# Attention ahead of a balanced mixture of experts: the order of tiles, q and loads, and where x waits

## The chip, the cores and the metric

The kernel runs on one core of one Trainium2 chip. The metric is the time of one execution on the device in microseconds (us), the median of several runs. Engines are named as in the profile: PE is TensorE (PEld its weight loads), ACT is ScalarE, DVE is VectorE, POOL is GpSimd, SP issues most of the DMAs.

## The reference

```
q, k, v: (8 batches, 8 heads, 576, 64) f32;  g_norm: (64,)
kv  = sum over s of k[s, d] v[s, e]              # per batch and head, 64 x 64
o   = q kv
x   = o / sqrt(mean(o*o over the head's 64) + 1e-6) * g_norm
x   -> (4608 tokens, 512): a token is (batch, s), its row the 8 heads side by side

logits = x w_gate                                # 8 experts
go through all (token, expert) pairs by falling logit; a token goes to the first
expert that still has room, each expert takes 4608 / 8 = 576 tokens
out[token] = relu(x[token] w1[e]) w2[e]          # w1: 512 x 1024, w2: 1024 x 512 per expert
```

## The kernel before

The work has three stages: the attention (to about 125 us), a search for the first expert's tokens (to about 160 us), and the eight experts, one after the other, with the search for the next ones beside them. The diff touches the first stage alone.

**Loads.** `load(name, b, h)` fetches one of k, v, q for batch `b` and half `h` of its heads, 576 KB (589,824 bytes), on SP's queue. Each name and half has two buffers, so a load for batch `b + 2` waits until PE has read the one of batch `b`. `paced` adds a dependence: a load or a write of x is not issued before the third one ahead of it has landed. SP issues in the order of the program. The first two batches are loaded at the start in the order k v q, k v q; later ones come from `again(names, h)` inside `prepare`.

**prepare(b)** is a generator that makes batch `b` ready in steps, which the tiles of batch `b - 1` are put between:

- `sum_kv(r)`: 18 products of 64 x 64 per pair of heads, into one PSUM tile `kv_ps`; ACT copies one half out (`odd`), DVE adds (`kv`), POOL copies it to both halves of `kvx`;
- `turn_q(n)`, n = 0 to 4: four blocks of q (two for n = 4) are transposed by PE into a PSUM tile `qt_ps`; DVE copies n = 1 and 2 to `qt`, ACT the others;
- `t_ps`: kv transposed by PE, copied by ACT to `kvt`; `w_ps`: kv times g_norm and w_gate, copied by DVE into the last columns of `kvx`, so that one product gives the attention's output and its share of the logits.

`qt_ps`, `t_ps` and `w_ps` share two PSUM buffers (tag `tr`). `qt` and `kvx` have three buffers each in SBUF.

**ones(n)** issues n products of a bf16 tile of ones, 512 columns, into a PSUM tile that is written over afterwards; they compute nothing that is used. There are 18 at the start, 5 in the preparation of batch 0, two ahead of each later `sum_kv`, and in every batch one ahead of tile 0 and two ahead of tile 3.

**tiles.** Batch `b` has four tiles of 128 tokens, and the odd batches a fifth one, made of the last 64 tokens' blocks of both batches of the pair (its products write 64 partitions each, hence `o_ps` x32 in the profile, where other tiles show x16). `one(t, ...)` computes a tile: products of `qt` and `kvx` into `o_ps` (two PSUM buffers), ACT's square `sq` and copy `o_sb`, and DVE's sum `ms`. After a batch's tiles, `scale()` gives `inv`, and `logits()` the logits `lg` of its tokens. x itself (`xo` = `o_sb` times `inv`) is made by POOL, one operation per tile, if the tile is `own`, else by ACT in eight operations per tile, which the list `late` puts behind the whole attention. `last_own = GC - (R + 1) // 2` makes the last batch's five tiles the late ones. The writes of `xo` to `x_dram` are held in `writes` and issued when eight or more are waiting; `xo` has five buffers.

**chores** are pieces of DVE work for the search (its constants, then for each quarter of the tokens `mx`, `pick`, `code_mx`, `best` and the comparison `over_c`), put in one by one after some tiles and at the end of a batch.

The order on PE, DVE, ACT and SP in this stage is that of the program (`manual_schedule`). The search that follows is a serial chain of DVE comparisons and PE counts (`given_ps`). At its end come the list of the first expert's tokens (`rel_s`, `ids`) and POOL's gather `xg` of their rows from `x_dram`. POOL's order is written out too: a small gather `rows_first` stands ahead of it, which waits for the last write of x.

Of the kernel before, what the change touches and what calls it, by code (L numbers as in the profile page):

```python
# [7 lines left out]
FT = mybir.dt.float32  # L8
# [7 lines left out]
P = 128  # L16
# [10 lines left out]
def kernel(  # L27
# [14 lines left out]
    B, H, S, D = q.shape  # L42
# [4 lines left out]
    HP = P // 2  # L47
    R = S // HP
# [39 lines left out]
            loaded[name, b, h].rearrange("p r j d -> p r (j d)"),  # L88
            src[b].rearrange("h s d -> (h s) d").rearrange("(r p j) d -> p r (j d)", r=NP, j=R)[:, rs]))

    for b in range(2):
        for h in range(2):
            for name in "kvq":
                load(name, b, h)

    ones_b = asg.tile([P, P], BF, name="ones_b")
    nc.vector.memset(ones_b, 1.0)
# [254 lines left out]
    def chore(times=1):  # L352

        for _ in range(times):
            if chores:
                chores.pop(0)()
# [12 lines left out]
    def prepare(b):  # L369

        k_sb, v_sb, q_sb = ([loaded.pop((name, b, h)) for h in range(2)] for name in "kvq")
        q_sb = [x.rearrange("p r j d -> p (r j d)") for x in q_sb]
        NT = NP * R // 2
        qt = att.tile([P, 2, NT, HP], FT, name="qt", tag="qt", bufs=3)
        turned_q[b] = qt

        def turn_q(n):
            m = min(4, NT - 4 * n)
            t_ps = psa.tile([P, 4, P], FT, name="qt_ps", tag="tr", bufs=2)
            for x in range(m):  # L380
                h, at = divmod(4 * n + x, NT // 2)
                nc.tensor.transpose(t_ps[:, x, :], q_sb[h][:, at * P:(at + 1) * P], ident)  # L382

            to, got = qt[:, :, 4 * n:4 * n + m], t_ps[:, 0:m].rearrange("p x (l c) -> p l x c", l=2)
            if n in (1, 2):
                nc.vector.tensor_copy(to, got)
            else:
                nc.scalar.copy(to, got)


        kv_ps = psa.tile([P, 2, 512], FT, name="kv_ps", tag="kv")

        def sum_kv(r):
            for j in range(R):
                for l in range(2):
                    ls, cs = slice(l * D, (l + 1) * D), slice(j % 2 * D, (j % 2 + 1) * D)
                    nc.tensor.matmul(kv_ps[cs, l, r * D:(r + 1) * D], lhsT=k_sb[r // 2][ls, r % 2, j, :], rhs=v_sb[r // 2][ls, r % 2, j, :],  # L397
                                     start=(j < 2), stop=(j >= R - 2))

        def again(names, h):  # L400
            if b + 2 < B:
                for name in names:
                    load(name, b + 2, h)

        if b > 0:
            ones(2, kv_ps[:, 0, :])
        for r in range(2):
            sum_kv(r)
            if r:
                again("kv", 0)  # L410
            turn_q(r)
            yield
        sum_kv(2)
        sum_kv(3)
        again("kv", 1)
        odd = att.tile([D, 2, NP * D], FT, name="odd", tag="odd")
        nc.scalar.copy(odd, kv_ps[D:P, :, 0:NP * D])
        kv = att.tile([D, NP, 2, D], FT, name="kv", tag="kv")
        nc.vector.tensor_tensor(kv.rearrange("p r l d -> p l r d"),  # L419
                                kv_ps[0:D, :, 0:NP * D].rearrange("p l (r d) -> p l r d", d=D),  # L420
                                odd.rearrange("p l (r d) -> p l r d", d=D), op=AL.add)

        kvx = att.tile([P, H, W], FT, name="kvx", tag="kvx", bufs=3)
        for n in range(2):
            nc.gpsimd.tensor_copy(kvx[n * D:(n + 1) * D, :, 0:D], kv.rearrange("p r l d -> p (r l) d"))  # L425
        if b == 0:
            ones(5)
        yield
        turn_q(2)
        again("q", 0)  # L430
        t_ps = psa.tile([P, NP, D], FT, name="t_ps", tag="tr", bufs=2)
        for r in range(NP):
            nc.tensor.transpose(t_ps[:, r, :], kv[:, r].rearrange("p l d -> p (l d)"), ident[0:D, 0:D])
        kvt = att.tile([P, NP, D], FT, name="kvt", tag="kvt")
        nc.scalar.copy(kvt, t_ps)
        yield
        turn_q(3)
        if b == 0:
            nc.vector.tensor_scalar(gw.rearrange("p r l e -> p (r l e)"), in0=gw.rearrange("p r l e -> p (r l e)"),
                                    scalar1=g_col, scalar2=None, op0=AL.mult)  # L440
        w_ps = psa.tile([P, NP, 2 * E], FT, name="w_ps", tag="tr", bufs=2)
        for r in range(NP):
            for n in range(2):
                nc.tensor.matmul(w_ps[n * D:(n + 1) * D, r], lhsT=kvt[:, r, :],
                                 rhs=gw[:, r].rearrange("p l e -> p (l e)"), start=True, stop=True)
        nc.vector.tensor_copy(kvx[:, :, D:W], w_ps.rearrange("p r (l e) -> p (r l) e", l=2))
        kv_of[b] = kvx
        turn_q(4)
        again("q", 1)

    LAG = 4
    writes, late = [], []
    last_own = GC - (R + 1) // 2

    def tiles(c0, rows):


        T = len(rows)
        o_sb = att.tile([P, T, H, W], FT, name="o_sb", tag="o_sb", bufs=2)
        xo = att.tile([P, T, H, D], FT, name="xo", tag="xo", bufs=LAG + 1)  # L460
        ms = att.tile([P, T * H], FT, name="ms", tag="ms")
        rt = att.tile([P, T * H], FT, name="rt", tag="rt")
        inv = att.tile([P, T * H], FT, name="inv", tag="inv")
        own = c0 + T <= last_own

        def one(t, copies, fill):

            o_ps = psa.tile([P, 2, 512], FT, name="o_ps", tag="o", bufs=2)
            ones(fill, o_ps[:, 0, :])
# [16 lines left out]
            sq = att.tile([P, H, D], FT, name="sq", tag="sq")  # L486
            nc.scalar.activation(sq.rearrange("p (b h) d -> p b h d", b=2), o4[:, :, :, 0:D], ACT.Square, scale=D ** -0.5)  # L487
            copies.append(lambda: nc.scalar.copy(o_sb[:, t].rearrange("p (b h) w -> p b (h w)", b=2), o_ps[:, :, 0:NP * W]))  # L488
            if own or t != T - 2:
                while copies:  # L490
                    copies.pop(0)()
            nc.vector.reduce_sum(out=ms[:, t * H:(t + 1) * H], in_=sq, axis=AXX)  # L492
# [38 lines left out]
    with tc.manual_schedule(engines={PE, DVE, ACTE, SPE}):  # L531
        ones(18)
        for _ in prepare(0):
            pass
        for b in range(B):
            parts = prepare(b + 1) if b + 1 < B else iter(())
            rows = [((b, j), (b, j + 2)) for j in (0, 1, 4, 5)]
            if b % 2:
                rows.append(((b - 1, R - 1), (b, R - 1)))
            one, scale, logits = tiles(b // 2 * R + b % 2 * (R // 2), rows)  # L540
            copies = []
            if b in choose_at:
                early(*choose_at[b])
            for t in range(len(rows)):
                one(t, copies, {0: 1, 3: 2}.get(t, 0))
                next(parts, None)
                if b < 2 or t == 3 or b == 6 and t == 2:
                    chore()
            for _ in parts:
                pass  # L550
            if b + 1 == B:
                while chores:
                    chore()
            scale()
            logits()
            if b < B - 1:
                chore(2 if b == 6 else 1)

            while len(writes) >= 2 * LAG:
                writes.pop(0)()  # L560
        early(27, GC)
        while chores:
            chore()
        for do in late:
            do()
        while writes:
            writes.pop(0)()
# [765 lines left out]
```

## Time and profile before

| | |
|---|---|
| median of 3 runs | 655.35 us (655.14 to 655.75) |
| the profiled execution | 656.87 us, its span 655.1 us |
| mean granted clock of PE | 0.964 |
| PE busy | 607.8 us, 93% of the span |
| DVE, POOL, ACT busy | 59%, 60%, 30% |
| moved by DMA | 91.02 MB, 139 GB/s over the span |
| last o_ps of the attention | 122.51 us |
| first gather of x (xg) | 155.30 us |

The profile is of one execution, by the hardware profiler. Its page gives the busy share of each engine in 40 slices of the span (a digit is tenths), the clock that PE was granted, the DMA engines' share, and the chain of work that ended last. The trace behind it gives timelines: start and length in us, the operation, and in brackets how long the engine had been idle before it and what ended that. A line with xN stands for N instructions; an f32 product of the program shows as two of them.

### The profile page before, as it was taken

How to read it: one execution, taken by the hardware profiler on the slowest of the kernel's cores; microseconds unless marked ns; L12 is line 12 of the kernel's file. 1: busy time of each engine (PE TensorE's matmuls, PEld its weight loads, DVE VectorE, ACT ScalarE, POOL GpSimd, SP SyncE). 2: the span in 40 equal slices, each digit the busy share in tenths (PEclk: the TensorE clock that was granted, in tenths of full speed). 3: DMA queues.
4: the chain of work that ended last, by engine and by line, in shares of the span. 5: the costliest groups of instructions: out<-in, count | busy, mean ns of one | idle time of the engine just before them, and what ended most of it. 6: DMA issues, size and time to landing. Idle time of an engine off the chain costs nothing.

```text
span 655.1 us, 12759 instructions
## 1 busy us (share of the span) xinstructions
PE 607.8 (93%) x4922; PEld 467.4 (71%) x4939; DVE 385.8 (59%) x1242; ACT 195.0 (30%) x397; POOL 391.1 (60%) x407
## 2 busy tenths in 40 slices
PE   7889999346999999999999999999999999999994
PEld 4767777343778678867877786778678867877873
DVE  4456767877788678578747955975771153123101
ACT  1545556631331223123212322221223123222310
POOL 1134544204586488659747973887388579848822
PEclk9979999756999999999999999999999999999998
DMA  8998988324506403620631082109104520820001
GB/s 271 315 313 293 309 300 320 126 83 144 185 2 232 137 34 109 220 74 1 213 125 66 2 291 70 42 5 325 41 33 128 203 72 1 292 77 34 0 10 64
DMA packets 49884, 91.02 MB, mean 139 GB/s; under 512 B 3744, under 2 KB 20128, under 8 KB 49824
## 3 DMA queue, kind: packets, MB, share of 16 engines
q1 hardware_dynamic: 43200, 71.31, 31.8%
q0 software_dynamic: 5920, 18.88, 8.4%
q8 instruction: 39, 0.64, 0.4%
q14 instruction: 21, 0.17, 0.1%
q10 hardware_dynamic: 704, 0.02, 0.1%
HBM read 71.32 MB, written 18.87 MB: 138 GB/s over the span
## 4 chain that ended last, share of the span: by engine, by line
PE 77%; DVE 8%; DMA 6%; issue 4%; ACT 2%; POOL 1%; POOLq 0%; SPq 0%; DVEq 0%; ACTq 0%
PE x_ps L1149 13%; PE x_ps L1109 12%; PE z_ps L1149 9%; PE y_ps L1149 9%; PE y_ps L1109 8%; PE z_ps L1109 7%; DMA v_sb<-in_v_dram 4%; PE o_ps L481 4%; PE y_ps L1211 4%; PE t_ps L1051 3%; PE kv_ps L397 3%; PE qt_ps L382 2%; PE given_ps L658 1%; PE given_ps L653 1%; DMA q_sb<-in_q_dram 1%
## 5 line engine op out<-in xcount | busy, mean ns | idle before, releaser
L1154 ACT COPY h<-x_ps 128x288 f32<-128x288 f32 x93 | 37.2, 400 | 166.1 <-PE x_ps L1149 159.7
L1149 PE MATMUL x_ps<-xs,sw 128*128 128x288 f32 x248 | 71.4, 409 | 0.4 <-DVE xs L1064 0.4
L1076 POOL DMA_INDIRECT out_dram<-y_sb,outs x32 | 31.5, 983 | 56.6 <-DVE y_sb L1247 41.1
L1109 PE MATMUL x_ps<-tw,sh 128*128 128x256 f32 x256 | 61.5, 384 | 0.0
L1149 PEld LDWEIGHTS x_ps<-xs,sw 128*128 128x128 f32 x248 | 46.1, 190 | 13.4 <-issue 1.0
L1056 ACT ACTIVATE xt<-t_ps,g_col 128x512 f32<-128x512 f32 (+3 forms) x41 | 25.8, 635 | 91.1 <-PE t_ps L1051 90.9
L1101 POOL TENSOR_TENSOR sh<-hid 128x512 f32<-128x512 f32 x32 | 40.7, 1273 | 19.9 <-ACT hid L1124 19.9
L1109 PEld LDWEIGHTS x_ps<-tw,sh 128*128 128x128 f32 x256 | 47.0, 190 | 7.0 <-issue 0.8
L1037 POOL TENSOR_TENSOR sw<-w_sb 128x256 f32<-128x256 f32 x64 | 46.8, 731 | 7.9 <-PE z_ps L1149 7.5
L513 POOL TENSOR_TENSOR xo<-o_sb,inv 128x512 f32<-128x512 f32 x31 | 32.9, 1091 | 30.7 <-DVE inv L500 17.5
L1124 ACT ACTIVATE hid<-hid 128x576 f32<-128x576 f32 x64 | 43.8, 686 | 22.6 <-DVE hid L1163 12.6
L959 POOL DMA_INDIRECT xg<-x_dram,ids x40 | 37.9, 947 | 15.5 <-issue 9.8
L481 PE MATMUL o_ps<-kvx,qt 64*128 64x72 f32 (+1 forms) x640 | 39.7, 273 | 5.3 <-ACT o_sb L488 3.4
L1187 POOL TENSOR_TENSOR tw<-w_sb 128x512 f32<-128x512 f32 x32 | 40.1, 1277 | 6.5 <-DMA w_sb<-in_moe_w_dram 6.5
L481 PEld LDWEIGHTS o_ps<-kvx,qt 64*128 64x128 f32 (+1 forms) x640 | 34.4, 180 | 12.9 <-issue 8.1
L1149 PE MATMUL z_ps<-xt,sw 128*128 128x288 f32 x128 | 38.0, 414 | 0.0
L1149 PE MATMUL x_ps<-xt,w_sb 128*128 128x288 f32 x124 | 37.3, 415 | 0.5 <-ACT xt L1056 0.5
L1149 PE MATMUL y_ps<-xt,w_sb 128*128 128x288 f32 x128 | 36.8, 408 | 0.0
L1149 PE MATMUL z_ps<-xs,sw 128*128 128x288 f32 x128 | 36.8, 409 | 0.0
L1149 PE MATMUL y_ps<-xs,w_sb 128*128 128x288 f32 x128 | 36.5, 407 | 0.0
L492 DVE TENSOR_REDUCE ms<-sq 128x8 f32<-128x512 f32 x36 | 24.3, 682 | 20.4 <-ACT sq L487 20.1
L425 POOL COPY kvx<-kv 64x512 f32<-64x512 f32 x16 | 9.7, 608 | 44.2 <-DVE kv L419 24.7
(307 smaller groups left out, 1336.1 us busy)
## 6 DMA issues: line engine op xcount, KB each, us to landing
w_sb<-in_moe_w_dram SPq DMA_DIRECT2D x32, 512.0 KB, 5.5
w_sb<-in_moe_w_dram SPq DMA_DIRECT2D x8, 2048.0 KB, 12.6
k_sb<-in_k_dram SPq DMA_DIRECT2D x16, 576.0 KB, 5.5
v_sb<-in_v_dram SPq DMA_DIRECT2D x16, 576.0 KB, 5.9
q_sb<-in_q_dram SPq DMA_DIRECT2D x16, 576.0 KB, 5.6
x_dram<-xo SPq DMA_DIRECT2D x16, 512.0 KB, 4.3
x_dram<-xo SPq DMA_DIRECT2D x4, 256.0 KB, 3.7
xg<-x_dram,ids POOLq DMA_INDIRECT x40, 5.0
```

Source lines behind the costliest of these rows:

```text
L481: nc.tensor.matmul(o_ps[rows_at, rp, (2 * r2 + l) * W:(2 * r2 + l + 1) * W], lhsT=turned_q[bn][ks, l, block // 2:block // 2 + m].rearrange ...
L513: nc.gpsimd.tensor_tensor(xo[:, t], o_sb[:, t, :, 0:D], inv[:, t * H:(t + 1) * H].rearrange("p (h o) -> p h o", o=1).to_broadcast([P, H, D ...
L959: tokens = nc.gpsimd.indirect_dma_start(out=xg[0:nr], out_offset=None, in_=x_dram, in_offset=bass.IndirectOffsetOnAxis(ap=ids[0:nr, n:n + ...
L1037: in_order(nc.gpsimd.tensor_tensor(o, x, y, op=op))
L1076: put = nc.gpsimd.indirect_dma_start(out=out, out_offset=bass.IndirectOffsetOnAxis(ap=ids_of[t][0:nr, n:n + 1], axis=0), in_=y_sb[0:nr, :] ...
L1101: in_order(nc.gpsimd.tensor_tensor(o[:, ms], x[:, ms], y[:, ms], op=op))
L1109: nc.tensor.matmul(p_ps[:, n], lhsT=left[:, f, n * P:(n + 1) * P], rhs=right[:, f], start=first, stop=(f == FH - 1), skip_group_check=True)
L1124: nc.scalar.activation(both, both, ACT.Relu)
L1149: nc.tensor.matmul(p_ps, lhsT=lhs[:, r], rhs=rhs[:, r], start=(m in (1, 2, 4, 5) and r == 0), stop=(r == 1), skip_group_check=(m in (6, 7, ...
L1154: nc.scalar.copy(u, p_ps)
L1187: in_order(nc.gpsimd.tensor_tensor(o, x, y, op=AL.subtract))
L1211: nc.tensor.matmul(y_ps[l * nr:(l + 1) * nr], lhsT=hid[:, l * FH + f, a:a + nr], rhs=w2[:, l * FH + f, :], start=(f == 0), stop=(f == FH - 1))
```

## The change

- The second batch's loads come in the order k v k v q q. In `prepare`, q is turned one step later than before (for b > 0): the sums of two pairs of heads fill the first step, group 0 of q comes in the second, groups 1 and 2 right behind `t_ps` in the third, 3 and 4 around `w_ps`. As before, the loads of q are asked for after groups 2 and 4.
- In odd batches the short tile, which also reads the batch before, goes first. `qt` and `kvx` get two buffers instead of three.
- Ones: in tiles only one each ahead of the first and the fourth tile of batches 0 to 2. In the preparation of batch 0 there are 8 more, in that of the last batch 3.
- x: `xo` has six buffers instead of five. The writes of batches 0 to 4 are issued together at the end of batch 4, behind all loads, those of batch 5 at its end, the rest after the attention. `last_own` makes batch 6 late too, so ACT makes nine tiles of x instead of five, POOL 27 instead of 31.
- The chores are put elsewhere: in batch 6 one after every tile, so that none is left for batch 7; in batches 2 to 5 after the second and fourth tile, and at the end of a batch only up to batch 3.

```diff
--- before.py
+++ after.py
@@ -88,10 +88,9 @@
             loaded[name, b, h].rearrange("p r j d -> p r (j d)"),
             src[b].rearrange("h s d -> (h s) d").rearrange("(r p j) d -> p r (j d)", r=NP, j=R)[:, rs]))
 
-    for b in range(2):
-        for h in range(2):
-            for name in "kvq":
-                load(name, b, h)
+    for b, order in enumerate(("kvqkvq", "kvkvqq")):
+        for n, name in enumerate(order):
+            load(name, b, int(name in order[:n]))
 
     ones_b = asg.tile([P, P], BF, name="ones_b")
     nc.vector.memset(ones_b, 1.0)
@@ -371,7 +370,7 @@
         k_sb, v_sb, q_sb = ([loaded.pop((name, b, h)) for h in range(2)] for name in "kvq")
         q_sb = [x.rearrange("p r j d -> p (r j d)") for x in q_sb]
         NT = NP * R // 2
-        qt = att.tile([P, 2, NT, HP], FT, name="qt", tag="qt", bufs=3)
+        qt = att.tile([P, 2, NT, HP], FT, name="qt", tag="qt", bufs=2)
         turned_q[b] = qt
 
         def turn_q(n):
@@ -402,14 +401,25 @@
                 for name in names:
                     load(name, b + 2, h)
 
+        turns = [[0], [1], [2], [3], [4]] if b == 0 else [[], [0], [1, 2], [3], [4]]
+
+        def turn_some():
+            for n in turns.pop(0):
+                turn_q(n)
+                if n in (2, 4):
+                    again("q", n // 2 - 1)
+
         if b > 0:
             ones(2, kv_ps[:, 0, :])
-        for r in range(2):
-            sum_kv(r)
-            if r:
-                again("kv", 0)
-            turn_q(r)
-            yield
+        sum_kv(0)
+        sum_kv(1)
+        again("kv", 0)
+        if b == 0:
+            ones(2)
+        turn_some()
+        yield
+        if b == 0:
+            ones(6)
         sum_kv(2)
         sum_kv(3)
         again("kv", 1)
@@ -420,21 +430,23 @@
                                 kv_ps[0:D, :, 0:NP * D].rearrange("p l (r d) -> p l r d", d=D),
                                 odd.rearrange("p l (r d) -> p l r d", d=D), op=AL.add)
 
-        kvx = att.tile([P, H, W], FT, name="kvx", tag="kvx", bufs=3)
+        kvx = att.tile([P, H, W], FT, name="kvx", tag="kvx", bufs=2)
         for n in range(2):
             nc.gpsimd.tensor_copy(kvx[n * D:(n + 1) * D, :, 0:D], kv.rearrange("p r l d -> p (r l) d"))
+        turn_some()
         if b == 0:
             ones(5)
         yield
-        turn_q(2)
-        again("q", 0)
+        if b + 1 == B:
+            ones(3)
         t_ps = psa.tile([P, NP, D], FT, name="t_ps", tag="tr", bufs=2)
         for r in range(NP):
             nc.tensor.transpose(t_ps[:, r, :], kv[:, r].rearrange("p l d -> p (l d)"), ident[0:D, 0:D])
         kvt = att.tile([P, NP, D], FT, name="kvt", tag="kvt")
         nc.scalar.copy(kvt, t_ps)
+        turn_some()
         yield
-        turn_q(3)
+        turn_some()
         if b == 0:
             nc.vector.tensor_scalar(gw.rearrange("p r l e -> p (r l e)"), in0=gw.rearrange("p r l e -> p (r l e)"),
                                     scalar1=g_col, scalar2=None, op0=AL.mult)
@@ -445,25 +457,24 @@
                                  rhs=gw[:, r].rearrange("p l e -> p (l e)"), start=True, stop=True)
         nc.vector.tensor_copy(kvx[:, :, D:W], w_ps.rearrange("p r (l e) -> p (r l) e", l=2))
         kv_of[b] = kvx
-        turn_q(4)
-        again("q", 1)
-
-    LAG = 4
+        turn_some()
+
+    HELD = 6
     writes, late = [], []
-    last_own = GC - (R + 1) // 2
+    last_own = GC - R
 
     def tiles(c0, rows):
 
 
         T = len(rows)
         o_sb = att.tile([P, T, H, W], FT, name="o_sb", tag="o_sb", bufs=2)
-        xo = att.tile([P, T, H, D], FT, name="xo", tag="xo", bufs=LAG + 1)
+        xo = att.tile([P, T, H, D], FT, name="xo", tag="xo", bufs=HELD)
         ms = att.tile([P, T * H], FT, name="ms", tag="ms")
         rt = att.tile([P, T * H], FT, name="rt", tag="rt")
         inv = att.tile([P, T * H], FT, name="inv", tag="inv")
         own = c0 + T <= last_own
 
-        def one(t, copies, fill):
+        def one(t, copies, fill, wait):
 
             o_ps = psa.tile([P, 2, 512], FT, name="o_ps", tag="o", bufs=2)
             ones(fill, o_ps[:, 0, :])
@@ -486,7 +497,7 @@
             sq = att.tile([P, H, D], FT, name="sq", tag="sq")
             nc.scalar.activation(sq.rearrange("p (b h) d -> p b h d", b=2), o4[:, :, :, 0:D], ACT.Square, scale=D ** -0.5)
             copies.append(lambda: nc.scalar.copy(o_sb[:, t].rearrange("p (b h) w -> p b (h w)", b=2), o_ps[:, :, 0:NP * W]))
-            if own or t != T - 2:
+            if not wait:
                 while copies:
                     copies.pop(0)()
             nc.vector.reduce_sum(out=ms[:, t * H:(t + 1) * H], in_=sq, axis=AXX)
@@ -541,10 +552,11 @@
             copies = []
             if b in choose_at:
                 early(*choose_at[b])
-            for t in range(len(rows)):
-                one(t, copies, {0: 1, 3: 2}.get(t, 0))
+            order = range(len(rows)) if b % 2 == 0 else [len(rows) - 1] + list(range(len(rows) - 1))
+            for n, t in enumerate(order):
+                one(t, copies, 1 if b < 3 and n in (0, 3) else 0, b + 1 == B and n == len(rows) - 2)
                 next(parts, None)
-                if b < 2 or t == 3 or b == 6 and t == 2:
+                if b < 2 or b == 6 or n in (1, 3):
                     chore()
             for _ in parts:
                 pass
@@ -553,10 +565,10 @@
                     chore()
             scale()
             logits()
-            if b < B - 1:
-                chore(2 if b == 6 else 1)
-
-            while len(writes) >= 2 * LAG:
+            if b < 4:
+                chore()
+
+            while b in (B - 4, B - 3) and writes:
                 writes.pop(0)()
         early(27, GC)
         while chores:
```

## The prediction

> **What bounds the kernel now.** I read the slices first, then the chain of waits in order of time over the attention, then PE's, DVE's and ACT's timelines at its two ends. All the diff's edits lie in the first 130 us, so what they are worth is read there.
>
> ```profile
> PEclk9979999756999999999999999999999999999998
> DMA  8998988324506403620631082109104520820001
> ```
>
> One slice is 16.4 us. DMA is near full in the first seven, while q, k and v come in, but it is not what ends them: from 36 us on the chain consists of PE pieces. PEclk has one dip to 7 inside the attention (slice 3), and a long one while the first experts' tokens are searched for (slices 8 to 10). The chain at that dip:
>
> ```profile
> 30.89 4.93 DMA q_sb<-in_q_dram
> 35.96 0.63 PE qt_ps L382 x4
> 36.59 1.04 PE o_ps L481 x16
> 37.63 0.96 PE kv_ps L397 x36
> 38.59 1.04 PE qt_ps L382 x4
> 39.64 1.92 PE o_ps L481 x16
> 41.55 2.33 PE kv_ps L397 x72
> ```
>
> The reader sees one load of q ending PE's wait, and then the same kinds of work taking almost twice their usual time (o_ps x16 is 1.04, then 1.92). PE's timeline puts the wait at 1.48 us, and the view by windows shows the clock:
>
> ```profile
> 37.00:38.00 1.00, 1.00 (x40) 0.98 0.93 334
> 38.00:39.00 1.00, 1.00 (x26) 0.50 1.01 369
> ```
>
> It stays at 0.50 to about 44.8. In the rest of the attention PE has two kinds of wait per pair of batches:
>
> ```profile
> 86.77 0.66 PE L382 MATMUL qt_ps<-ident,q_sb 128*128 128x128 f32 x4 [0.52 <-ACT kvt L435]
> 101.16 0.44 PE L382 MATMUL qt_ps<-ident,q_sb 128*128 128x128 f32 x2 [0.41 <-DVE kvx L446]
> ```
>
> At the attention's end another engine sets the pace; DVE's timeline and PE's last tile:
>
> ```profile
> 117.39 1.11 DVE L305 TENSOR_TENSOR best<-pick,code_mx 128x72 bf16<-128x72 f32 x1
> 118.42 2.22 DVE L337 TENSOR_TENSOR over_c<-mx,cand 128x192 bf16<-128x192 f32 x2
> 120.56 2.08 DVE L492 TENSOR_REDUCE ms<-sq 128x8 f32<-128x512 f32 x3
> ...
> 122.51 0.73 PE L481 MATMUL o_ps<-kvx,qt 64*64 64x72 f32 x32 [2.98 <-ACT o_sb L488]
> ```
>
> The last tile waits 2.98 us for a PSUM bank, whose copy stands on ACT behind a square, which waits for a reduction that DVE gets to only at 120.56. After 125 us a serial search follows (DVE, PE, DVE), to the gather of x at 155.30, and then the experts for 500 us. The diff leaves both alone, so a gain at 125 us comes through whole, if x is in memory by then.
>
> **The change part by part.** Tile loop b starts (first o_ps of batch b) at 32.10, 49.69, 62.37, 75.43, 88.68, 101.74 and 114.43 for b = 1 to 7.
>
> *Batch 1: loads as k v k v q q, and q turned one step later.* Before, batch 1 takes 49.69 − 32.10 = 17.59 us; batch 3, with the same work, 13.06. The 4.5 us are 1.48 of waiting and about 3.0 of slow clock (36.52 to 44.78 is 8.26 us; the same pieces from 65.27 to 70.52 take 5.25). After, batch 2's k, v are summed, then a tile, sums, and only then q is turned: from 32.1, short tile 0.70, two ones 0.54, sums 1.31, a fill 0.27 at most, tile 1.05, sums 1.31 give 37.2, while that q load landed at 35.9. For batch 1 the two q loads come two places later; SP's issue times (a load is issued when the third before it has landed) put the tenth and eleventh landing at 24.4 and 26.4, and PE turns them at about 25 and 27. So the cover is 0.5 to 1.3 us, thin: if it fails, a wait below 1 us comes back. By work, batch 1 is four tiles 4.20, a short one 0.70, sums 2.62, turning 2.66, t_ps 0.39, w_ps 0.65, four ones 1.08, and 1.0 of waits (below): 13.3. Gain 4.3.
>
> Here a rule of the Trainium skill speaks against me. "TensorE: Matmul & The Clock Gate", in its part on what is actually happening, has the clock halved after at least one idle window of some 3.4 us. By that a wait of 1.48 us halves nothing, the dip has another cause and stays, and the gain of this part is 4.3 − 3.0 = 1.3. The trace: the clock falls at 38.0 and is back at 44.8, two such windows, and the one that ends at 38.0 holds the wait of 1.48, 43% of it. Counted back in steps of 3.4 us, the one that ends at 14.1 holds a wait of 1.04 (30%), and the clock stays at 1.00. So I take a partly idle window as enough, and 4.3; the rule's value is the lower end.
>
> *Few ones.* The page's 61 ones become 54: 18 fills in tiles go (one each in batches 0 to 2, three each in 3 to 7), 11 come (8 in batch 0's preparation, under its waits for loads of 0.69 and 1.04; 3 in the last). Two ones take 0.54 in the chain, so 13 fills in batches 2 to 6 are 3.5 us of PE.
>
> *What takes their place.* t_ps is now followed at once by two turned groups that share two PSUM buffers. The second needs t_ps's, which ACT frees after sq 0.50, o_sb 0.53 and kvt 0.39, some 1.55 after the tile before; PE gets there after t_ps 0.39 and one group 0.59. A wait of 0.6 in every batch, and 0.4 on kvx at the last group: 1.0 per batch, where before it was 0.41 (odd) or 0.5 to 0.7 (even). By work an odd batch is then 11.76 + 1.0 = 12.8, an even one 12.1 (b = 2, with two fills, 12.6; b = 6 has three ones in the place of a wait, 12.3): 62.5 for batches 2 to 6 against 114.43 − 49.69 = 64.7. Of these 2.3 us, 0.6 is a single slow o_ps in batch 4 (1.69 against 1.11) that the diff does not touch. Gain 1.7.
>
> *Short tile first, two qt and kvx instead of three.* Now batch b + 1 overwrites what batch b − 1 left; its last reader is the short tile, done 0.8 us into the batch. POOL writes kvx some 6 us in and the first turned group comes at 5: covered. Nothing else is queued behind POOL's wait but xo.
>
> *Chores moved.* DVE's last comparison (best, two over_c) now runs in batch 6, at its end, where POOL no longer scales x. Then it costs what it does alone (best 0.23 to 0.30; over_c 0.45 for all 288 at 129.39) or at most what it did beside POOL. From batch 7's start S: comparison to S + 1.0, the scales and logits of batch 6 2.15 (115.01 to 117.16), so the first reduction ends at S + 3.8, sq and o_sb at 4.9, last tile to 6.1, square and two copies to 7.9. Before it was 124.98 − 114.43 = 10.55. Gain 2.6; if over_c stays slow, 1.7.
>
> *x held, batch 6's x on ACT.* The 20 writes remain 20. Three that stood before batch 7's loads on SP (80.55 to 86.1) now come after all loads, twelve in a row from about 92; 9.4 MB at 310 GB/s is 30 us, done by 122 but for the last two batches. Those wait for ACT: 72 multiplications instead of 40, at 9.66/40 = 0.24 us, 17.4. They start after the last square root, 125.2 − 8.6 = 116.6, to 134.0; the last write lands 3.9 later (before: 136.1 to 140.0), at 138. Behind ACT's multiplications stands only the copy for the token list, due at 152.39 − 8.6 = 143.8; behind the last write on SP the expert's index, due at 150.25 − 8.6 = 141.7; POOL's warm-up gather waits for that write, and nothing else on POOL is due before rel_s, 153.40 − 8.6 = 144.8. Cost zero with 7 us of cover; at the row's 0.334 each it would still be just in time. POOL loses four xo, 4.2 us that nobody waits for.
>
> Sum: 4.3 + 1.7 + 2.6 = 8.6. Span 655.1 − 8.6 = 646.5; the profiled execution's own time is 656.87, 1.5 above the median of the runs, 655.35, so it would be 648.3, and the median 646.8.
>
> **The rivals.** *The dip stays* (by the rule above, or because another load is late by 1 us): the gain is 8.6 less 3.0 to 4.3, time 649.8 to 651.1. For it: thin cover at 25 and 36 us. *The clock drops without fills* (the slower side): in batches 3 to 7 a window of 3.4 us with 1.0 us of waits more often falls under the gate. A spell costs 3.0 as at 38; it decides from the third, four of them give 655.35 − 8.6 + 12 = 658.8. For it: waits double in odd batches. Against: from 77.1 to 83.0 there is not one fill and the clock reads 1.00, and the two waits are 4 us apart, so no window has over 0.7 idle. *x comes late*: with x 10 us later than reckoned, 3 beyond its cover, 649.8; ACT's 0.24 each and the trace's DMA gaps after 116 us speak against it. *Nothing reaches the end* (a hidden wait elsewhere): 655.
>
> **How the numbers follow.** Forecast 0.75, the dip stays 0.11, the clock drops 0.07, x late 0.03, nothing 0.04. The forecast's own range is 645 to 648.5, from tail 1.7 to 3.4 and steady part 1.1 to 2.3. To 651.5 it takes in the first rival and x late. About 0.2% (1.3 us) is what can be told from no change: faster 0.89, same 0.04, slower 0.07.
>
> **What would show it.** Right: no clock below 1.00 from 14 to 110 us; batch 1 at 13.3; waits of 0.6 on ACT kvt and 0.4 on DVE kvx in each batch; batch 7 from 108.5; first search matmuls near 116.5; gather near 146.7; ACT's xo to 134 and the last x landed before 140. Wrong: a slice with PEclk at 7 or 8 in the attention, PE waiting for q_sb, or xg waiting for x_dram.

## The result, and the profile after

The changed kernel takes 651.53 us, median of 22 runs (649.01 to 665.93), the kernel before 656.3 (22 runs, 653.52 to 668.98). The ratio is 0.9921, 95% interval 0.9902 to 0.9939: faster by 0.8%, some 5.2 us. Ratios, here and below, leave out the runs that lie more than 1.5% above the fastest of their kernel, so they are not quite those of the medians. The forecast was faster by 8.6 us, to 646.8. So the sign was right and the size too large by 3.4 us. The profiled execution of the changed kernel took 650.66 us, its span is 648.9; before had 656.87 and 655.1.

The clock by slices, from the page after:

```profile
PEclk9999999559999999999999999999999999999998
```

The 7 that stood in slice 3 is gone, and the long dip of the search, which ran to slice 10, is over after slice 9. The view by windows (stretch, length, busy time of PE, PEld, DVE, ACT and POOL with their instructions, granted clock, DMA share, GB/s) of the changed kernel for 14 to 110 us:

```profile
14.00:110.00 96.00, 86.15 (x1909) 71.35 (x1920) 61.07 (x170) 56.21 (x111) 38.27 (x43) 1.00 0.91 305
```

The clock is 1.00 throughout, as forecast. PE's timeline of the changed kernel (start, length, operation, idle time before it and what ended that) at the places the prediction named, and at two that it did not (24.73 and 91.70):

```profile
24.73 1.03 PE L396 MATMUL kv_ps<-v_sb,k_sb 64*64 64x64 f32 x48 [0.66 <-issue]
...
41.36 0.66 PE L381 MATMUL qt_ps<-ident,q_sb 128*128 128x128 f32 x4 [0.62 <-ACT kvt L446]
...
58.49 0.44 PE L381 MATMUL qt_ps<-ident,q_sb 128*128 128x128 f32 x2 [0.39 <-DVE kvx L458]
...
91.70 1.06 PE L381 MATMUL qt_ps<-ident,q_sb 128*128 128x128 f32 x7 [0.55 <-issue]
...
113.61 1.44 PE L492 MATMUL o_ps<-kvx,qt 64*128 64x72 f32 x16 [0.38 <-ACT o_sb L499]
...
116.81 0.87 PE L665 MATMUL given_ps<-best,over_c 128*32 128x8 bf16 x27 [1.76 <-ACT o_sb L499]
```

The waits of 0.62 and 0.39 are the forecast's 0.6 and 0.4. The last tile waits 0.38 for its PSUM bank instead of 2.98, and the search's first products come at 116.81 (forecast 116.5, before 125.03). The line at 24.73 shows 0.66 us of "issue", time in which PE waited for nothing that the profile shows, in the middle of 72 products of the same kind. The line at 91.70 is a second such gap, at a place where PE waits for kvt in the other batches. DVE's, ACT's and POOL's timelines of the changed kernel:

```profile
108.29 0.23 DVE L304 TENSOR_TENSOR best<-pick,code_mx 128x72 bf16<-128x72 f32 x1
108.43 0.52 DVE L336 TENSOR_TENSOR over_c<-mx,cand 128x192 bf16<-128x192 f32 x2
...
116.86 17.28 ACT L529 ACTIVATE xo<-o_sb,inv 128x64 f32<-128x64 f32 x72
...
137.05 1.17 POOL L886 DMA_INDIRECT rows_first<-x_dram,iota_p_i  x1 [30.60 <-DMA x_dram<-xo]
```

The comparison costs 0.75 us where it cost 3.3; ACT's x runs to 134.1 and the last x has landed by 137.05, almost eleven us ahead of the gather at 147.88.

Read by stages, this pair of executions answers to the forecast: 8.2 of the 8.6 us are there at 116.81. Of these the gather keeps 7.4 (one count of the search took 0.8 longer), the experts' first products 7.2, and the end 6.2 (among the experts PE stood for 0.49 us of "issue" ahead of a product at 205.72 and waited 0.18 us ahead of one at 451.53; the rest of this 1.0 was not traced). The timed runs say 5.2. So either the losses on the way are part of the kernel and a little more is lost in most runs, or before's profiled execution was not a typical one.

### The profile page after: what moved, and what is told of

It is laid out like the page before. It is cut to its first block, busy times and chain, and to the rows that moved or that the text cites. A ratio compares the mean times of both kernels' runs of the same rounds, so it can differ in the third digit from the quotient of the medians.

```text
span 648.9 us, 12775 instructions
## 1 busy us (share of the span) xinstructions
PE 601.2 (93%) x4918; PEld 464.2 (72%) x4932; DVE 380.6 (59%) x1242; ACT 202.3 (31%) x429; POOL 387.0 (60%) x403
## 4 chain that ended last, share of the span: by engine, by line
PE 78%; DVE 8%; issue 5%; DMA 4%; ACT 3%; POOL 2%; POOLq 0%; SPq 0%; DVEq 0%; ACTq 0%
PE x_ps L1161 13%; PE x_ps L1121 12%; PE z_ps L1161 9%; PE y_ps L1161 9%; PE y_ps L1121 8%; PE z_ps L1121 7%; PE o_ps L492 4%; PE y_ps L1223 4%; PE t_ps L1063 3%; DMA v_sb<-in_v_dram 3%; PE kv_ps L396 2%; PE qt_ps L381 2%; PE given_ps L670 1%; PE given_ps L665 1%; ACT sq L498 1%
## 5 line engine op out<-in xcount | busy, mean ns | idle before, releaser
L1161 PEld LDWEIGHTS x_ps<-xs,sw 128*128 128x128 f32 x248 | 46.1, 190 | 13.3 <-issue 0.9
L524 POOL TENSOR_TENSOR xo<-o_sb,inv 128x512 f32<-128x512 f32 x27 | 28.4, 1081 | 40.3 <-DVE inv L511 40.3
L1161 PE MATMUL y_ps<-xs,w_sb 128*128 128x288 f32 x128 | 36.5, 407 | 0.0
L1253 ACT COPY u<-x_ps 128x512 f32<-128x512 f32 x24 | 14.0, 584 | 67.3 <-PE x_ps L1121 52.6
```

The lines of the kernel that those rows point to most:

```text
L524: nc.gpsimd.tensor_tensor(xo[:, t], o_sb[:, t, :, 0:D], inv[:, t * H:(t + 1) * H].rearrange("p (h o) -> p h o", o=1).to_broadcast([P, H, D ...
L1161: nc.tensor.matmul(p_ps, lhsT=lhs[:, r], rhs=rhs[:, r], start=(m in (1, 2, 4, 5) and r == 0), stop=(r == 1), skip_group_check=(m in (6, 7, ...
```

## The experiments

All times below are medians beside the kernel before on the same chip and in the same session; the chips differ by 0.3%, so ratios are compared.

**1. Batch 2's q asked for one place earlier, in the kernel before** (`b_qearly`): undoes the wait of 1.48 us for q, nothing else.

```
-        again("kv", 1)
+        if b > 0:
+            again("kv", 1)
...
         again("q", 0)
+        if b == 0:
+            again("kv", 1)
```

> The kernel before, with only the order of batch 2's loads changed: its first half of q is asked for ahead of the second half of k and v. Theory A (the wait for q of 1.48 us lets the clock fall): the wait at 34.5 us goes, PE's clock stays at 1.00 from 14 to 110 us, batch 1 takes about 13.2 us instead of 17.6, the time falls by about 4.4 us (ratio 0.993); the second half of k and v is needed at 37.2 and lands near 37.8, so up to 0.6 us may come back as a wait. Theory B (a fully idle window of some 3.4 us is needed, so the dip has another cause): the dip stays, only the wait goes, 1.3 to 1.5 us (ratio 0.998).

Measured: 653.82 against 654.53, ratio 1.0002 (0.9963 to 1.0041). Its profile has no dip, and a span of 650.9, 4.2 below that of before. A span that is 4.2 better and a time that is the same do not go together, unless before's profiled execution was not like its timed runs.

**2. Six ones under the wait for q, in the kernel before** (`b_fillwait`): keeps the wait, takes away PE's idleness in it.

```
             if r:
                 again("kv", 0)
+            if b == 2 and r == 0:
+                ones(6)
             turn_q(r)
```

> The kernel before, with six products of ones put on PE just ahead of the first turning of batch 2's q, where PE waits 1.48 us for the load: the wait for data stays, PE is not idle in it (six by 0.27 is 1.6 us). Theory A: no dip of the clock at 38 us; 36.5 to 44.8 becomes about 5.3 us instead of 8.3; gain 3.0 less 0.1 (ratio 0.9955). Theory B: the clock dips as before, nothing gained (ratio 1.000), or 0.1 lost.

Measured: 654.68, ratio 0.9992 (0.9959 to 1.0025); span 652.1, clock 1.00 to 110 us. The same riddle.

**3. The kernel before once more, and a third time** (`b_again`, `b_third`).

> The kernel before once more, unchanged: does the slow clock from 38.0 to 44.8 us, which the prediction counted as 3.0 us of gain, belong to the kernel or to the one execution that was profiled? Theory S (the clock falls only in some executions): this profile shows PEclk 1.00 from 14 to 110 us and a span near 652, and most of the timed runs have a mean clock of 0.967 to 0.971 where the profiled one had 0.964 (6.83 us at half clock are 0.005 of the mean). Theory K (the wait for q always lets the clock fall): a dip of 6.8 us near 38 us again, span 655, mean clock 0.964 in most runs. The time is that of the kernel before, ratio 1.000, either way.

> The kernel before a third time, one look: of its two profiled executions one had a wait of 1.48 us for q at 34.5 and 6.8 us of slow clock after it, the other a wait of 0.41 and none. If the wait belongs to the kernel and the second look was the exception: 1.4 us again, and a dip unless the wait lies across two windows of 3.41 us. If it was chance: below 0.6 us, PEclk 1.00 from 14 to 110, span 651 to 652.5.

Measured: 654.24 against 654.76, ratio 1.0012 (0.9975 to 1.0048), span 651.7; `b_third`, a single run, took 655.59, span 653.8. The wait for q in PE's timeline, of `b_again` and of `b_third`:

```profile
34.85 0.63 PE L382 MATMUL qt_ps<-ident,q_sb 128*128 128x128 f32 x4 [0.41 <-DMA q_sb<-in_q_dram]
```

```profile
35.53 0.63 PE L382 MATMUL qt_ps<-ident,q_sb 128*128 128x128 f32 x4 [1.04 <-DMA q_sb<-in_q_dram]
```

The clock by slices of `b_again`, with nothing below 9 in the attention (`b_third` has nothing either):

```profile
PEclk9999999657999999999999999999999999999998
```

The load is late by 0.41 to 1.48 us from one execution to the next, and in two of the three profiles of this kernel the clock does not fall. The timed runs point the same way, though less sharply. A spell of 6.83 us at half clock is 0.005 of the mean clock; the profile with the dip stands at 0.964, the two without at 0.967 and 0.970. Of the runs of before in the four sessions, 40 of 77 stand at 0.967 or more. The others may hold this spell or another loss: `b_qearly`, which has no such wait, has 5 of 12 lower too. So the slow spell that the forecast counted as 3.0 us is missing in about half of the executions, if not more, and with it the gain that experiments 1 and 2 were to show. Their intervals leave room for 2.4 and 2.7 us, not for the 4.4 and 2.9 expected.

**4. The changed kernel once more** (`a_again`).

> The changed kernel once more, beside the kernel before and two relatives on the same chip: which of the profiled execution's small losses (0.66 us of PE waiting for nothing at 24.7, 0.8 us in the sixth count at 138, 1.1 us in two places of the experts) come again? If they belong to the kernel: batch 1 from 33.2, gather at 147.9, span 648.9. If they are chance: batch 1 from 32.3, gather near 146.5, span near 647. Time ratio to before 0.992; under theory S (the clock falls before only in some executions) no better than 0.991, under theory K about 0.987 if the losses are chance.

Measured: 649.35, ratio 0.9908 (0.9874 to 0.9942), span 647.5. The 0.8 of the search and the gaps in the experts do not come again: chance. The stall in batch 0 does, with 1.00 us in the place of 0.66:

```profile
25.22 1.03 PE L396 MATMUL kv_ps<-v_sb,k_sb 64*64 64x64 f32 x48 [1.00 <-issue]
```

**5. The fills put back into the changed kernel** (`a_fills`).

```
-                one(t, copies, 1 if b < 3 and n in (0, 3) else 0, b + 1 == B and n == len(rows) - 2)
+                one(t, copies, {0: 1, 3: 2}.get(n, 0), b + 1 == B and n == len(rows) - 2)
```

> The changed kernel, with the ones in the tiles as they were before (one ahead of the first tile worked on, two ahead of the fourth, in every batch). If the fills were only a cost: 19 more by 0.27 us on PE in batches 0 to 7, of which some lie in waits; batch 7 starts 3.9 us later (near 112.7 instead of 108.8), ratio about 1.006 against the changed kernel, 0.998 against the one before. If they were what kept the clock up: PEclk is at 1.00 in the attention in both, so no gain can show. Rival: the fills lie in waits that are there anyway (0.62 and 0.39 per batch), and cost under 1 us.

Measured: 654.11, ratio 0.9994 (0.9958 to 1.0031). The gain is gone with them: against 0.9908 to 0.9921 this is about 5 us, known to 2.5 (forecast: 3.5 us of PE in batches 2 to 6, and their place in batch 7 besides). The profile shows what the products themselves cost: over batches 3 and 4, where it has no "issue" gap, they are 26.26 us where both profiles of the changed kernel have 24.92, so 1.34 for six ones. But it also has gaps of 1.57 us ahead of 38.91, 1.99 ahead of 95.98, with a dip of the clock behind it, and 0.73 ahead of 110.72, and more products move the places of such gaps (experiment 9). How the 5 us divide between the ones and the gaps is not shown. Without the fills' removal the rest of the change gains nothing that can be told.

**6. The chores of batch 6 put back** (`a_chores`).

```
-                if b < 2 or b == 6 or n in (1, 3):
+                if b < 2 or b == 6 and n > 1 or b != 6 and n in (1, 3):
                     chore()
...
-            if b < 4:
-                chore()
+            if b < 4 or b == 6:
+                chore(2 if b == 6 else 1)
```

> The changed kernel with the tail's chores put back as before: in batch 6 the first assignment's comparisons run only as two chores at the later tiles, so the last of them comes in batch 7 again. The prediction valued this move at 2.6 us (1.7 if the comparison stays slow). By it: batch 7 to first search matmul 10 to 10.6 us in the place of 8.0, a wait of about 3 us for the last o_sb copy, span 1.7 to 2.6 longer than the changed kernel, ratio to before 0.995 to 0.996. Rival: the last chore is hidden without it too, since the fills left batch 7: below 0.5 us, ratio 0.992.

Measured: 651.22 against 649.35 of `a_again` in the same session, ratio to before 0.9934 (0.9904 to 0.9963), where `a_again` has 0.9908. The intervals overlap; the profile shows the mechanism. PE's timeline, DVE's after it:

```profile
116.26 1.99 PE L492 MATMUL o_ps<-kvx,qt 64*128 64x72 f32 x16 [1.26 <-ACT o_sb L499]
120.01 0.88 PE L665 MATMUL given_ps<-best,over_c 128*32 128x8 bf16 x27 [1.77 <-ACT o_sb L499]
```

```profile
113.72 0.24 DVE L304 TENSOR_TENSOR best<-pick,code_mx 128x72 bf16<-128x72 f32 x1
113.87 0.52 DVE L336 TENSOR_TENSOR over_c<-mx,cand 128x192 bf16<-128x192 f32 x2
```

Batch 7 began at 110.55, so its tail is 9.46 us against 8.01 and 7.70 in the two profiles of the changed kernel: 1.5 to 1.8 more. Of this 0.9 is the longer wait for o_sb (1.26 against 0.38), and the rest is the clock, which had fallen at 116.1 (o_ps x16 in 1.99 us where `a_again` has 1.11). The comparison is not slow here (0.76 for both, 3.3 before), though it runs in batch 7: POOL multiplies no x then. In the kernel before, where the comparison ran from 117.39 to 120.6, it did:

```profile
116.27 4.25 POOL L513 TENSOR_TENSOR xo<-o_sb,inv 128x512 f32<-128x512 f32 x4 [4.07 <-ACT sq L487]
```

Another operation of the chores shows the same: `pick` takes 0.97 us at 104.34 in the changed kernel, beside POOL's multiplication, and 0.23 at 110.30 in `a_chores`, with POOL idle. So at this place it was POOL's multiplication beside it that made the comparison slow, and either part of the change takes that away: the x left to ACT here, the move in experiment 7.

**7. Batch 6's x on POOL again** (`a_own`): `last_own = GC - R` becomes `GC - (R + 1) // 2`.

> The changed kernel with batch 6's x scaled on POOL again, as before, in the place of ACT at the end: the prediction costed this part at nothing, with 7 us of cover. By it: ACT's multiplications 40 of 9.7 us in the place of 72 of 17.3, POOL's warm-up gather some 4 us earlier, the gather of x at 147 to 148 as in the changed kernel; ratio 0.991. Rival: POOL's x beside DVE's comparison in batch 6 makes that slow again (over_c 1.1 us each in the place of 0.26), the tail 0.5 to 1.5 us longer, ratio 0.993.

Measured: ratio 0.9884 (0.9796 to 0.9972, four runs), gather at 147.43. ACT's multiplications are 40 again, 9.65 us from 118.48. POOL's x:

```profile
111.43 4.14 POOL L524 TENSOR_TENSOR xo<-o_sb,inv 128x512 f32<-128x512 f32 x4 [4.41 <-ACT sq L498]
```

POOL starts x after the comparison, which here too is done in 0.75 us from 108.87. With the chores moved, giving this x to ACT costs and brings nothing that can be measured, as costed.

**8. q turned in pairs where two buffers are free** (`a_spread`, `a_spread2`): aimed at the two waits that the change brought in.

```
-        turns = [[0], [1], [2], [3], [4]] if b == 0 else [[], [0], [1, 2], [3], [4]]
+        turns = [[0], [1], [2], [3], [4]] if b == 0 else [[], [0, 1], [2], [], [3, 4]]
```

> The changed kernel, with q's groups spread so that two are turned in the second step, one behind the transposed kv, and the last two behind the gate's product. If the waits of 0.62 for kvt's copy come from two groups in a row on two PSUM buffers, they go in batches 1 to 5 (six by 0.6), the 0.39 stays: batch 7 starts 3.7 us earlier, near 105, and the ratio against the kernel before is about 0.987 if the changed kernel has 0.992. Rival: the loads are the bound by then (48 loads at 1.97 us end near 97), PE waits for q or k instead and under 1 us is gained.

> The changed kernel with q turned in pairs after the first and the fourth tile and singly after the second, once more and on the same chip as the changed kernel itself. If its time of 645.96 came from the two waits per batch (0.62 for kvt and 0.39 for kvx, 1.0 us in six batches) it is again 5 to 6 us below the changed kernel, ratio to before 0.984 to 0.987. If it came from the chip or from a run without stalls, it is within 2 us of the changed kernel.

Measured: 645.96 (ratio 0.9856, 0.9797 to 0.9915), then 645.41 (0.9855, 0.9814 to 0.9897) where `a_again` had 649.35. Five of the six runs of `a_spread2` lie below the fastest of the seven of `a_again` (647.42), and the two sessions agree: about 0.5% beyond the changed kernel, and the fastest version of this study. The wait for kvt is gone from the batches of the attention; that for kvx stays, here in a batch of `a_spread2`:

```profile
90.42 0.65 PE L456 MATMUL w_ps<-gw,kvt 128*64 128x16 f32 x16
91.00 0.66 PE L381 MATMUL qt_ps<-ident,q_sb 128*128 128x128 f32 x4
92.05 0.44 PE L381 MATMUL qt_ps<-ident,q_sb 128*128 128x128 f32 x2 [0.39 <-DVE kvx L458]
```

Batch 7 starts at 105.51 (`a_spread2`, in spite of 3.4 us of half clock from 25.0) and 106.16, where the changed kernel had 108.80 and 109.70.

**9. A longer program for PE** (`a_shift`, `a_pad`): 32 more products of 8 columns at the start, each with its weight load, under a wait for the first loads. `a_pad` adds them; `a_shift` puts 40 of them in the place of 8 ones.

```
         ones(18)
+        short = psa.tile([P, 512], FT, name="ones_ps", tag="tr", bufs=2)
+        for _ in range(32):
+            nc.tensor.matmul(short[:, :8], lhsT=ones_b, rhs=wide[:, :8], start=True, stop=True)
```

> The changed kernel with 40 matmuls of 8 columns in the place of 8 of the 18 ones at the start, under the wait for the first loads: 32 matmuls more in PE's program, nothing else. PE stood still for nothing that the profile shows (issue) at 24.1 to 24.7 or 25.2 us, always ahead of the last 48 of 72 kv_ps matmuls, and at 38 ahead of the last 60. Theory F (PE waits for its own program, fetched in blocks): the stall stays at the same place of the program, so it comes 32 matmuls earlier: between the eighth and the ninth of the 16 o_ps ahead of that group (at 23 us), and the second between the last four of the group before and its first 68, each 1.2 to 1.6 us after a packet of the instruction queue has landed. Theory D (a data wait that the profile does not name): it stays ahead of the last 48 kv_ps. Time within 0.3% of the changed kernel either way, ratio 0.991.

> The changed kernel with all of its 18 ones at the start and 32 matmuls of 8 columns after them: PE's program has the same length and the same contents at every place as in a_shift, but the start is as long a run of wide ones as in the changed kernel. It asks why a_shift took 1.0092 of the kernel before: where the program's blocks[...] end, or the weaker start. Theory P (the place: a block that ends in a batch's t_ps or behind a wait lets PE stand for its program and for kvt in one window of 3.41 us, and the clock falls): spells of half clock of 10 us or more near 68 and 99 us again, most runs with a mean clock below 0.960, ratio 1.000 to 1.010. Theory W (the start): no spell before 110 us, batch 1 no later than 34.5, mean clock 0.967 or more, ratio 0.990 to 0.993. In between (0.994 to 0.999): stalls for the program but fewer spells.

Measured: `a_shift` 664.37, ratio 1.0092 (1.005 to 1.0134); `a_pad` 666.46, ratio 1.0108 (1.0054 to 1.0162). The 32 products take 0.94 us in `a_pad`, at 7.01, and PE still waits for v at 12.79, where the changed kernel has that wait ended at 12.66. Yet by the ratios the kernel takes 11 to 12 us longer, where 0.3% was expected at most, and the gain of 0.8% becomes a loss of 1%. All ten timed runs of `a_shift` have a mean clock of 0.945 to 0.959, where 18 of the changed kernel's 22 are at 0.966 to 0.973. Theory P holds, and theory W falls: `a_pad`, with the start of the changed kernel, has spells of half clock too (from 25.2 and from 103.7, not near 68 and 99). PE's timeline of `a_pad` (only the place is read from it):

```profile
22.59 0.77 PE L492 MATMUL o_ps<-kvx,qt 64*128 64x72 f32 x9
26.04 1.13 PE L492 MATMUL o_ps<-kvx,qt 64*128 64x72 f32 x7 [2.68 <-issue]
```

The stall that stood ahead of the last 48 kv_ps now stands inside the 16 o_ps ahead of them, 24 + 7 = 31 products earlier, where theory F has 32 (the counts of products up to the gap are 343 and 344); no data comes in between the ninth and the tenth product of one tile. `a_shift` shows no gap at that place, and others later:

```profile
66.82 0.67 PE L492 MATMUL o_ps<-kvx,qt 64*128 64x72 f32 x7 [0.89 <-issue]
...
68.98 1.11 PE L381 MATMUL qt_ps<-ident,q_sb 128*128 128x128 f32 x4 [0.66 <-ACT kvt L446]
...
98.83 0.34 PE L396 MATMUL kv_ps<-v_sb,k_sb 64*64 64x64 f32 x6 [2.51 <-issue]
```

The windows of `a_shift` around these stalls show what the time went into:

```profile
65.21:68.63 3.42, 2.21 (x25) 1.87 (x24) 1.67 (x4) 1.75 (x5) 1.95 (x3) 1.00 0.85 308
68.63:72.04 3.41, 3.06 (x21) 2.60 (x22) 1.50 (x3) 0.29 (x2) 0.00 (x0) 0.50 0.86 245
95.93:99.35 3.42, 0.91 (x32) 0.71 (x25) 0.62 (x1) 0.56 (x2) 1.51 (x2) 1.00 1.05 401
```

A stall of 0.89 and the wait for kvt lie in one window of 3.4 us; the clock then stays at half for four such windows (13.65 us from 68.63), and for five (17.07 us from 99.35) behind the second stall. That the place of the stalls makes the clock fall in all of these runs is concluded from one profile of each kernel and the mean clocks of the timed runs.

## Why the prediction was right or wrong, point by point

The marks below are from two profiled executions each: before without the dip (`b_again`, `b_third`), after its first profile and `a_again`.

| Mark, us | before, without the dip | after | gain | forecast |
|---|---|---|---|---|
| batch 1 begins | 32.06, 32.11 | 33.25, 33.60 | −1.3 | 0 |
| batch 1 | 13.51, 14.14 | 13.31, 13.87 | 0.2 | 4.3 |
| batches 2 to 6 | 64.93, 65.27 | 62.24, 62.23 | 2.9 | 1.7 |
| batch 7 to the search | 11.11, 11.10 | 8.01, 7.70 | 3.2 | 2.6 |
| sum | | | 5.0 | 8.6 |

The sum is close to the 5.2 us of the timed runs. Put on the forecast's 655.35, the ratio gives 650.2: outside the 645 to 648.5 of the forecast itself, and inside the 649.8 to 651.1 where it put its first rival, that the dip stays. That it landed there is luck: the clock does not fall in either profile of the changed kernel, and about half of the executions before have no dip that could stay.

*Batch 1: the step that failed.* The 13.3 us after were right (13.31; 13.87 has 0.32 of "issue" in it). Wrong was the 17.59 us before, taken from one execution as if the kernel always took it. The 3.0 of slow clock and part of the wait of 1.48 (0.41 and 1.04 in the other two) belong to that execution. The working "batch 3, with the same work, 13.06" stood beside it in the prediction; with a short wait for q it is the usual length of batch 1 (13.51 and 14.14), and the 4.5 us above it were a loss whose frequency was unknown.

*The rule of the clock.* The Trainium skill's "TensorE: Matmul & The Clock Gate", in its part on what is actually happening, asks for an idle window of some 3.4 us; the forecast put a partly idle window in its place. On that the runs side with the forecast: the clock fell behind windows with PE busy for 2.00 us (before), 1.42 (`a_fills`), 2.35 (`a_spread2`) and 2.21 (`a_shift`) of 3.41, none of them idle. But the sum of idleness alone does not decide: `a_spread` stood still for 2.35 us from 36.5 to 38.9 and kept its clock, with PE busy for 2.22 and 2.26 in the two windows that the wait lies across, and with 2.37 `b_third` kept it too. Between 2.2 and 2.4 it goes both ways, and the same wait can be split by the border of two windows or not. So the rule is too strict for these runs. The forecast's own reading, a partly idle window as enough, was right, but no ground for counting the dip in every execution; the rule's value for this part, 1.3, lies nearer to the measured 0.2 than 4.3 does. The two windows of `a_spread`:

```profile
34.29:37.71 3.42, 2.22 (x76) 1.94 (x68) 3.35 (x14) 1.30 (x3) 3.42 (x4) 1.00 0.94 317
37.71:41.12 3.41, 2.26 (x70) 2.03 (x72) 0.67 (x2) 1.02 (x2) 0.66 (x1) 1.00 0.96 314
```

*Batch 0: a cost that was missing.* The forecast let batch 1 begin where it began before. It begins 1.3 us late, for the most part because of the "issue" gap at 24 us, present in the first profile of the changed kernel and in five of six of `a_again` and the relatives with the same start (0.53 to 1.00 us). The sixth, `a_chores`, has no gap there and begins batch 1 at 32.48, still 0.4 late. In the first profile PE also waits 0.20 us for q_sb at 25.96: a sign of being wrong by the forecast's list, of the size (below 1 us) that it allowed for. The Trainium skill's "Runtime: NRT & Kernel Launch", in its part on instruction fetch mechanics, has the program come in blocks of 256 instructions and calls the cost of crossing into the next one mostly hidden. Here it is not always hidden. The count of PE's products and weight loads up to the gap, from windows of the changed kernel that end at the gap:

```profile
0.00:24.70 24.70, 19.78 (x343) 12.71 (x347) 10.28 (x51) 7.48 (x12) 2.49 (x10) 1.00 0.85 283
0.00:91.65 91.65, 79.62 (x1733) 62.95 (x1745) 53.30 (x178) 47.10 (x90) 33.02 (x44) 1.00 0.91 301
```

and of `a_shift`:

```profile
0.00:66.80 66.80, 58.30 (x1227) 45.32 (x1237) 36.94 (x143) 30.92 (x58) 20.42 (x30) 1.00 0.92 311
0.00:98.81 98.81, 85.31 (x1734) 68.05 (x1745) 51.65 (x175) 45.06 (x86) 31.96 (x42) 0.93 0.90 305
```

343 + 347 is 690; 3478 in the changed kernel and 3479 in `a_shift` are the same count at different operations. From 690 on, 3478 is 11 steps of 253.5 counted instructions, and 2464 is 7 of 253.4. If two or three in each block are of a kind that the profile does not count, such a step is a block of 256; this is read from the counts, the trace does not say it. The kernel before has such gaps too, in `b_again` and in `b_third`, with 2462 and 3474 counted up to them, again 7 and 11 steps of 253:

```profile
69.41 0.53 PE L481 MATMUL o_ps<-kvx,qt 64*64 64x72 f32 x18 [0.51 <-issue]
```

```profile
94.60 0.45 PE L481 MATMUL o_ps<-kvx,qt 64*128 64x72 f32 x4 [0.58 <-issue]
```

In the trace each of these gaps ends 1.2 to 1.6 us after a packet of the instruction queue has landed. In the view of DMA queues for 22.1 to 23.6 us of the changed kernel (packets, MB, share of the engines) that packet stands among the loads:

```profile
q1 hardware_dynamic: 216, 0.47, 90.5%
q8 instruction: 1, 0.02, 5.4%
```

Why the changed order shows a gap at the count of 690 and the old one none was not tried.

*Steady part.* 62.5 forecast, 62.24 and 62.23 measured, with the waits of 0.62 and 0.39 where they were forecast. (64.74 less 62.5 is 2.2, where the forecast has 2.3.) The gain is larger than 1.7 because of what the kernel before loses besides. It took 64.74 in its first profile, 64.93 in `b_again` and 65.27 in `b_third`; without single losses it is 64.2 in all three. The first holds the slow o_ps that the forecast set aside (0.6), `b_again` the gap ahead of 69.41 (0.75 with what it split), `b_third` the one ahead of 94.60 (0.8) and a slow o_ps (0.3). The changed kernel's gap of 0.55 ahead of 91.70 cost nothing, since it took the place of a wait for kvt: its batches 5 and 6 are as long as those of `a_again`, which has no gap there. So 1.9 of the 2.9 are work and waits, near the forecast, and 1.0 is such losses, of which the forecast counted none. Two profiles of each do not show that the changed kernel is spared them as a rule.

*Tail.* 7.9 forecast, 8.01 and 7.70 measured. The kernel before took 10.60 by this mark in its first profile and 11.1 in the other two, where the clock had fallen before the last tile (1.24 us in the place of 0.73). Putting the comparison back costs 1.5 to 1.8 by experiment 6, below the forecast's 2.6, since x on ACT alone already makes it fast; 0.9 of that is waiting, the rest where the clock fell. What remains of the gain would have to come from the fills that left batch 7 and the order of tiles; they were not tried apart.

*x.* Cost zero, cover 7 us: `a_own` and the landing by 137.05 bear it out.

*The rivals.* "The clock drops without fills" did not happen to the changed kernel, but `a_shift` and `a_pad` show that it was nearer than 0.07: its argument against, "no window has over 0.7 idle", left out that PE also waits for its program. The price of a spell was also well above the 3.0 that it was given: 30.7 us at half clock in two spells of `a_shift`, some 13 us by the forecast's own 3.0 for 6.83 (an estimate).

## What to carry to other kernels

A loss that one profiled execution shows is worth its size times how often it happens: profile a second execution, or compare the mean clock of the timed runs, before its removal goes into a sum. When filler work is taken out, count every kind of idleness that can fall into one clock window, "issue" gaps too, since a few small waits together cost whole windows at half clock. And when a change lengthens or shortens an engine's program ahead of a stretch that is full of DMA, expect the stalls at its block ends to move, and measure the neighbours (a few instructions more) before trusting a gain below 1%.

## What the runs showed of the hardware that was not expected

- PE stands still for 0.2 to 2.7 us at places of its program that lie 253 to 254 counted instructions apart, or a multiple of that, while the DMA engines are near full (shares of 0.85 to 1.05 above): the same count in different kernels, not at every such place, and not in every execution.
- A spell of half clock lasts whole windows of 3.41 us: one (`a_fills`, `a_spread2`), two (before), four and five (`a_shift`), six (`a_pad`). What makes it last longer than one, while PE in before and `a_shift` is busy for 3.06 us and more of each, stays open.
- Some DVE operations take several times as long beside POOL's multiplication (the comparison 3.3 us in the place of 0.75, `pick` 0.97 in the place of 0.23); others do not (`code_mx` 0.28 at 117.08 before, 0.27 at 107.03 after).
- 32 products of 8 columns at the start move the whole kernel by 1.9% (ratio 0.9921 to 1.0108), more than twice the change that this study is about.
